# Later places for the steps of an attention unit, and smaller, spread loads of the down stage's tables, in a pooled-attention and two-MLP kernel

## The chip, the cores and the metric

The kernel runs on one core of a Trainium2 chip. The metric is device time in microseconds, here 1985.22 us as the median of three runs. A core has five engines with one instruction queue each, and each queue is worked off in order: TensorE (PE, with its weight loads as PEld), VectorE (DVE), ScalarE (ACT), GpSimd (POOL) and SyncE (SP), which only issues DMAs here. An instruction that waits holds up everything behind it on its own engine.

## The reference

```
k_p, v_p = mean over 8 neighbouring keys        # 576 -> 72 keys, 8 batches x 8 heads, 64 wide
a = softmax(q @ k_p.T / 8);  x = a @ v_p        # x: 4608 tokens x 512
h = x @ w_in;  g = h * clip(h + 3, 0, 6) / 6    # w_in 512 x 2048
y = g @ w_out                                   # w_out 2048 x 512
out = (silu(y @ w_gate) * (y @ w_val)) @ w_out2 # 512 x 1536, 1536 x 512
```

Everything is float32; the weights come as 64-bit numbers that the kernel converts itself.

## The kernel before

A float32 product is made of three products of rounded parts: each operand is split into a high part (rounded by ACT) and a remainder (a subtraction by DVE).

The program has three stages. The **up stage** handles 9 blocks of 512 tokens. A block has 16 feature tiles f; each is one group of 12 matmuls (`up`, L579) into one of three PSUM buffers, an activation (`act1`: ACT `t`, DVE `g`, for f < 8 also GpSimd), and a store of g (256 KB) to DRAM (`store_g`). The **down stage** (L838, 63 products in a seven-product scheme) reads g and seven tables of w_out, 2 MB each (`load_pw`), and the **last stage** (L663 and behind) does the second MLP.

While block j runs in the up stage, the attention of block j+1 is computed between the groups of matmuls, and the attention of block 0 runs ahead of them. So blocks 0 to 7 carry attention, and block 8 carries none. Attention is cut into 96 units (a head pair and up to 256 queries). The steps of a unit are letters:

- S: scores on PE into PSUM (`pss`), row maximum on DVE. X (`exps`): DVE subtracts the maximum into the tile `e`, and ACT takes the exponential. N: DVE adds the rows up and inverts the sums. M: GpSimd multiplies them in. E: ACT rounds the last columns into `et`, and DVE (odd units) or GpSimd (even ones) subtracts.
- T: PE transposes into PSUM (`pst`, two buffers). U: ACT rounds that into `aT`, `aTt`. L: DVE makes the remainder.
- V: four products on PE into `psv`, which has one buffer. W: ACT rounds it into `x`. Y: DVE makes the remainder, which frees `psv` for the next unit's V.
- Per head: RK and K (pooled keys, by GpSimd and then PE and ACT), R0, R1 and R (pooled values). Per segment of queries: P.

A table `when` gives each step a pair (d, p): unit i does it in unit interval i + d, at place p of the interval. All steps are sorted by that into one list, `steps`. The list is cut in front of its S, V and T steps into 30 pieces per block, and two pieces follow each group of 12 matmuls: one ahead of `act1`, one behind it (`attn_slot`). Each engine's queue is written in this order. Where blocks 0 and 1 are concerned (`early_units`), ACT subtracts the maximum itself. At the end of feature tiles, `prep_slot` adds the preparation of later tables, 20 of them within blocks 1 to 7: for each, at the ends of several feature tiles, ACT rescales, DVE joins halves of words, GpSimd adds (L202), ACT rounds (L261), DVE subtracts (L264).

In the last block the loads for the down stage are put on SP's queue ahead of the block's first group: g of block 0 (4 pieces of 1 MB) and two tables; four more tables follow at f = 3, 7, 11 and 15, the last at the end. The stores of g stand on the same queue.

Of the kernel before, what the change touches and what calls it, by code (L numbers as in the profile page):

```python
# [9 lines left out]
F32R = mybir.dt.float32r  # L10
# [8 lines left out]
def f32(ap):  # L19
    return ap.bitcast(F32)  # L20
# [3 lines left out]
def kernel(  # L24
# [27 lines left out]
    nc = tc.nc  # L52
# [227 lines left out]

    attn_ctx = ExitStack()
    a_p = attn_ctx.enter_context(tc.tile_pool(name="a", bufs=1, side="right"))
    NE = 2
    MAXQ = 2
    QJ = N // P
    kbd_t = [a_p.tile([P, K2], F32, name=f"kbd{p}") for p in range(KT)]
# [172 lines left out]
        qT_t[seg] = t.rearrange("p c s -> p (c s)")  # L459

    n_unit = [0]
    s_t, ps_t, x_ps = {}, {}, {}

    def scores(u):
        b, p, s0, n, qt = u
# [14 lines left out]
    def exps(u):  # L480
        b, p, s0, n, qt = u
        ni = n // qt
        g = ni * 2
        s3, mx, st = s_t.pop(u)
        if st:
            e = es_t[0][:, MAXQ * K2 * (n_unit[0] % 3):][:, :MAXQ * K2]
            e = e.rearrange("q (i s) -> q i s", i=MAXQ)[:qt, :ni]
        else:
            e = a_p.tile([P, MAXQ, K2], F32, tag="e", name="e", bufs=NE)[:qt, :ni]
        e3 = e.rearrange("q i (h s) -> q (i h) s", h=2)  # L490
        sm = a_p.tile([P, 2 * MAXQ, 1], F32, tag="sm", name="sm", bufs=3)[:qt, :g]
        if u in early_units:
            for i in range(g):
                nc.scalar.activation(
                    out=e3[:, i], in_=s3[:, i], func=ACTF.Exp, bias=mx[:, i], accum_out=sm[:, i]
                )
        else:
            nc.vector.tensor_tensor(  # L498
                out=e3, in0=s3, in1=mx.to_broadcast([qt, g, SP_]), op=ALU.subtract
            )  # L500
            nc.scalar.activation(out=e, in_=e, func=ACTF.Exp)  # L501
        e_t[u] = (e, e3, et_t[n_unit[0] % NE][:qt, :ni], sm)
        n_unit[0] += 1

    def normalise(u):
        _, e3, _, sm = e_t[u]
# [87 lines left out]
            nc.gpsimd.tensor_tensor(out=g[:, MB:], in0=g[:, :MB], in1=g[:, MB:], op=ALU.subtract)  # L594
        return g

    def store_g(j, f, g):
        nc.sync.dma_start(out=g_d[j][:, :, f // NP1, f % NP1], in_=g.rearrange("p (r n) -> p r n", r=2))

# [200 lines left out]
            t = gq[j, slot] = lb["gq"].tile([P, NP1, MB], F32, tag=f"gq{slot}", name="gq")  # L800
            nc.sync.dma_start(out=t, in_=g_d[j][:, r, c])

    def load_pw(n, tile_of):
        what = DN[n][2]
        t = tile_of("pw")
        lb["pw", what] = t.rearrange("p (f a n) -> p f a n", f=NP1, a=2)
        nc.sync.dma_start(out=f32(t), in_=s_w1[:, B7[what]].rearrange("p f a n -> p (f a n)"))

    SLOT = {"11": 0, "S1": 0, "12": 1, "S4": 1, "S3": 2, "22": 3, "S2": 3}

# [74 lines left out]
    for j in range(NB):  # L885
# [28 lines left out]

    when_startup = {
# [3 lines left out]
    }  # L919
    when = {  # L920
# [3 lines left out]
    }  # L924
    events = []
    for i in range(NU):
        startup_unit = i < unit_end[0]
        lag = dict(when_startup if startup_unit else when)
        if 0 <= i - unit_end[0] < NE:
            lag["E"] = (1, 22)  # L930
        if i == unit_end[0]:
            lag["V"], lag["W"] = (3, 10), (3, 11)
        stages = [(what, i) for what in "SXNMETULVWY"]
        if 2 <= i < 8:
            stages.append(("C", i))
        if i in first_in_seg:
            stages.append(("P", first_in_seg[i]))
        if i in first_in_head:
            stages += [(what, first_in_head[i]) for what in ("RK", "K", "R0", "R1", "R")]
        events += [(i + lag[st[0]][0], lag[st[0]][1], st[1], st) for st in stages]  # L940
    steps = [e[3] for e in sorted(events, key=lambda e: e[:3])]
    block_end = [1 + steps.index(("Y", e - 1)) for e in unit_end]


# [11 lines left out]

    for i, u in enumerate(units):
        h, sg = head_no[u[:2]], seg_no[seg_of[u]]
        before(*((what, i) for what in "SXNMETULVWY"))
        before(("P", sg), ("S", i))  # L960
        before(("RK", h), ("K", h), ("S", i))
        before(("R0", h), ("R", h), ("V", i))
        before(("R1", h), ("R", h))
        if i + 1 < NU:
            for what in "SXE":
                before((what, i), (what, i + 1))
        if h + 4 < len(heads):
            before(("S", i), ("K", h + 4))
            before(("V", i), ("R", h + 4))
        if h + 1 < len(heads):  # L970
            before(("K", h), ("RK", h + 1))
        if h + 2 < len(heads) and h >= KT - 1:
            before(("R", h), ("R1", h + 2))
        in_startup = at["S", i] < block_end[0]
        ring(*(("h", 3) if in_startup else ("att", 2)), ("S", i), ("X", i))
        assert not in_startup or at["X", i] < block_end[0]
# [6 lines left out]
        ring("mx", 2, ("S", i), ("X", i))  # L983
        ring("sm", 3, ("X", i), ("M", i))
# [16 lines left out]
    def do_step(st):  # L1001
        what, i = st
        if what == "RK":
            if i not in pe_pooled:
                reduce_k(*heads[i])
                next_k(i)
        elif what == "K":
            transpose_k(*heads[i])
            if i in pe_pooled:
                next_k(i)  # L1010
        elif what == "R0":
            prep_v(*heads[i])
        elif what == "R1":
            pool_v(vt_t[heads[i]])
        elif what == "R":
            split_v(*heads[i])
            for h in ((KT, KT + 1) if i == KT - 1 else (i + 2,)):
                if KT <= h < len(heads) and i >= KT - 1:
                    load_vtail(*heads[h], nc.sync)
            for h in ((KT, KT + 1) if i == KT - 1 else (i + 2,)):  # L1020
                if KT <= h < len(heads) and i >= KT - 1:
                    load_v(*heads[h], nc.sync)
        elif what == "P":
            prep_q(segs[i])
            for n in ((KT, KT + 1) if i == KT - 1 else (i + 2,)):
                if KT <= n < len(segs) and i >= KT - 1:
                    later.append((done[0] + 12, lambda n=n: load_q(segs[n], sync4)))
        elif what == "S":
            scores(units[i])
        elif what == "N":  # L1030
            normalise(units[i])
        elif what == "X":
            exps(units[i])
        elif what == "M":
# [28 lines left out]
    with tc.manual_schedule():  # L1063
# [43 lines left out]
        def load_next():  # L1107

            if sent[0] < NG * len(stream):
                kind, what = stream[sent[0] % len(stream)]  # L1110
                (load_up if kind == "up" else load_dn)(what)
                sent[0] += 1

        for j in range(NB):
            for f in range(F1):
                if (j, f) == (NB - 1, 0):
                    attn_ctx.close()
                    for nm in ("gq", "px"):
                        lb[nm] = right_b.enter_context(
                            tc.tile_pool(name=nm, bufs=1, side="right", reuse_waits="tile"))  # L1120
                    load_g(0, 0)
                    load_pw(0, lambda name: lb["px"].tile([P, BIG], F32R, tag="px", name=name))
                    load_pw(1, big_x)
                    for slot in (3, 2, 1):
                        load_g(0, slot)
                hp = ps_h.tile([P, N], F32, tag="h", name="h")
                up(hp, wu[f], x_tile(j))
                attn_slot(j, 2 * f)
                g = act1(f, hp)
                attn_slot(j, 2 * f + 1)  # L1130
                store_g(j, f, g)
                if j == 0:
                    weights.convert()
                else:
                    prep_slot(F1 * (j - 1) + f)
                if j == NB - 1:
                    if f % 4 == 3:
                        load_pw(2 + f // 4, big_w)
                    if 10 <= f < 10 + NCB:
                        split_b(0, f - 10)  # L1140
        load_pw(6, big_x)
        l1.close()
        l1_ps.close()
        lb["o"] = left_b.enter_context(tc.tile_pool(name="ob", bufs=1, reuse_waits="tile"))
# [91 lines left out]
```

## Time and profile before

| | us |
|---|---|
| median of 3 runs (1984.73 to 1987.58) | 1985.22 |
| the profiled execution: its time, its span | 1987.09, 1985.4 |
| up stage with attention, blocks 0 to 7 | 53.3 to 755.4 |
| up stage, block 8 | 755.4 to 818 |
| down stage and last stage | 818 to 1985.4 |

The stretches are read from the starts of the first groups of L579 in blocks 0 and 8, and from the first matmul of the down stage. Times in a trace count from the start of the span.

### The profile page before, as it was taken

The page shows a single profiled execution, that of the slowest core. Times are in us where ns is not written, and L with a number is a line of the kernel's source. Part 1 is how long each engine was busy: PE and PEld are TensorE (multiplying, and loading weights), DVE is VectorE, ACT ScalarE, POOL GpSimd, SP SyncE. Part 2 cuts the span into 40 slices and gives each one's busy share as a digit, 9 for nine tenths or more (in the row PEclk, how much of TensorE's full clock was granted, in tenths as well). Part 3 has the DMA queues.
Part 4 walks back from the last instruction along what each step waited for, and adds up shares of the span by engine and source line. Part 5 has one row for each costly group of instructions (what it writes and reads, how often), then busy time and mean ns, then how long its engine had stood idle before and what let it go on. Part 6 is the DMA issues. An engine that isn't in the chain of part 4 may idle for free.

```text
span 1985.4 us, 31395 instructions
## 1 busy us (share of the span) xinstructions
PE 1781.0 (90%) x11241; PEld 1663.1 (84%) x11241; DVE 1346.6 (68%) x2398; ACT 761.5 (38%) x1689; POOL 690.7 (35%) x898
## 2 busy tenths in 40 slices
PE   5877678786777876999999989999999999999999
PEld 4666566565656665999999989999999999999999
DVE  6666666665667652488788776676866867768666
ACT  5443334343434342445555542332422423324223
POOL 5436374646464431000000005515335155153360
PEclk8888989998988888999999999999999999999999
DMA  7635555756464648856455537788797787887876
GB/s 170 157 104 148 170 171 179 223 184 187 159 177 164 187 152 317 279 210 215 168 170 192 201 145 254 244 292 282 243 321 259 266 300 245 294 286 242 289 246 221
DMA packets 234828, 432.52 MB, mean 218 GB/s; under 512 B 86576, under 2 KB 168496, under 8 KB 218416
## 3 DMA queue, kind: packets, MB, share of 16 engines
q1 hardware_dynamic: 232528, 429.20, 65.0%
q8 instruction: 89, 1.46, 0.3%
q10 hardware_dynamic: 2144, 1.31, 0.2%
q14 instruction: 67, 0.55, 0.1%
HBM read 326.11 MB, written 104.33 MB: 217 GB/s over the span
## 4 chain that ended last, share of the span: by engine, by line
PE 69%; DVE 9%; DMA 6%; POOL 6%; ACT 6%; issue 4%; SPq 1%; POOLq 0%; DVEq 0%; ACTq 0%
PE b L663 40%; PE b L838 18%; PE h L579 9%; POOL e L514 2%; DMA g<-g 1%; DVE g L592 1%; DMA q_in<-in_q_dram 1%; ACT t L590 1%; DVE x L572 1%; DVE mx L477 1%; POOL vts L425 1%; DMA qv<-in_q_dram 1%; DVE sm L508 1%; POOL k_in L382 1%; ACT s L261 1%
## 5 line engine op out<-in xcount | busy, mean ns | idle before, releaser
L663 PE MATMUL b<-xc,wr 128*128 128x384 f32 x3024 | 529.5, 336 | 7.7 <-DMA wr<-sup 3.3
L663 PEld LDWEIGHTS b<-xc,wr 128*128 128x128 f32 x3024 | 527.2, 189 | 8.8 <-ACT xc L144 7.0
L579 PE MATMUL h<-x,wu 128*128 128x512 f32 x1728 | 477.6, 433 | 19.0 <-DVE g L592 16.9
L579 PEld LDWEIGHTS h<-x,wu 128*128 128x128 f32 x1728 | 355.2, 212 | 96.0 <-DVE g L592 17.9
L710 POOL TENSOR_TENSOR s<-s,c 128x384 f32<-128x384 f32 x144 | 142.4, 1014 | 763.3 <-ACT s L708 763.3
L672 DVE TENSOR_TENSOR c<-c,b 128x384 f32<-128x384 f32 x504 | 265.2, 552 | 179.0 <-PE b L663 155.3
L838 PEld LDWEIGHTS b<-gb,pw 128*128 128x128 f32 x3024 | 362.3, 191 | 0.4 <-DVE gb L145 0.2
L838 PE MATMUL b<-gb,pw 128*128 128x256 f32 x3024 | 362.6, 283 | 0.0
L663 PE MATMUL b<-wr,gc 128*128 128x256 f32 x2268 | 265.6, 279 | 0.0
L663 PEld LDWEIGHTS b<-wr,gc 128*128 128x128 f32 x2268 | 265.4, 188 | 0.0
L144 ACT CAST gb<-gq 128x512 fp32r<-128x512 f32 x252 | 155.9, 622 | 172.6 <-PE b L838 157.3
L145 DVE TENSOR_TENSOR gb<-gq,gb 128x512 fp32r<-128x512 f32 x252 | 168.6, 689 | 72.9 <-ACT gb L144 71.6
L717 POOL TENSOR_TENSOR gf<-s,c 128x384 f32<-128x384 f32 x144 | 168.3, 1193 | 66.9 <-DVE c L672 64.4
L592 DVE SCALAR_TENSOR_TENSOR g<-t,h 128x512 f32<-128x512 f32 x144 | 98.6, 685 | 134.0 <-ACT t L590 97.3
L144 ACT CAST gc<-gf 128x768 fp32r<-128x768 f32 x126 | 105.7, 839 | 186.9 <-POOL gf L717 101.0
L708 ACT ACTIVATE s<-c 128x384 f32<-128x384 f32 x144 | 73.5, 526 | 204.6 <-DVE c L672 203.3
L557 PE MATMUL psv<-aT,vst 128*128 128x256 f32 (+3 forms) x96 | 34.8, 362 | 123.7 <-DVE x L572 118.4
L514 POOL TENSOR_TENSOR e<-e,sm 96x288 f32<-96x288 f32 (+3 forms) x85 | 57.8, 680 | 251.4 <-DVE sm L510 221.5
L145 DVE TENSOR_TENSOR gc<-gf,gc 128x768 fp32r<-128x768 f32 x126 | 133.8, 1094 | 15.6 <-ACT gc L144 13.9
L557 PEld LDWEIGHTS psv<-aT,vst 128*128 128x128 f32 x96 | 20.9, 218 | 138.7 <-issue 61.4
L590 ACT ACTIVATE t<-h,half 128x512 f32<-128x512 f32 x144 | 99.0, 688 | 54.7 <-PE h L579 54.5
L501 ACT ACTIVATE e<-e 96x288 f32<-96x288 f32 (+3 forms) x76 | 31.4, 413 | 191.4 <-DVE e L498 191.4
(106 smaller groups left out, 1864.7 us busy)
## 6 DMA issues: line engine op xcount, KB each, us to landing
wr<-sup SPq DMA_DIRECT2D x72, 1024.0 KB
wr<-sdn SPq DMA_DIRECT2D x84, 768.0 KB
wr<-sup SPq DMA_DIRECT2D x72, 768.0 KB
g<-g SPq DMA_DIRECT2D x144, 256.0 KB
gq<-g SPq DMA_DIRECT2D x36, 1024.0 KB
sup<-s SPq DMA_DIRECT2D x12, 1792.0 KB
wstg<-in_moe_w_out_dram SPq DMA_DIRECT2D x56, 256.0 KB
sw<-s SPq DMA_DIRECT2D x8, 1792.0 KB
```

The costliest lines, as they stand in the source:

```text
L144: nc.scalar.copy(out=hi, in_=src)
L145: lo_engine.tensor_tensor(out=lo, in0=src, in1=f32(hi), op=ALU.subtract)
L514: nc.gpsimd.tensor_tensor(out=e3, in0=e3, in1=sm.to_broadcast(list(e3.shape)), op=ALU.mult)
L579: nc.tensor.matmul(out=ps, lhsT=w(kt, wh), rhs=x(kt, xh), start=first and n == 0, stop=last and n == 3 * len(kts) - 1,)
L590: nc.scalar.activation(out=t, in_=ps, func=ACTF.Relu, bias=half, scale=1.0 / 6.0)
L592: nc.vector.scalar_tensor_tensor(out=g, in0=t, scalar=1.0, in1=ps, op0=ALU.min, op1=ALU.mult)
L663: nc.tensor.matmul(out=ps, lhsT=w(wh), rhs=x(xh), start=first and n == 0, stop=last and n == 2)
L672: add = lambda dst, a, b: nc.vector.tensor_tensor(out=dst, in0=a, in1=b, op=ALU.add)
L708: nc.scalar.activation(out=g[q], in_=c[q], func=ACTF.Sigmoid)
L710: nc.gpsimd.tensor_tensor(out=g[q], in0=g[q], in1=c[q], op=ALU.mult)
L717: nc.gpsimd.tensor_tensor(out=gf[p][:, GP[TURN[q]], f], in0=g[q], in1=c[q], op=ALU.mult)
L838: nc.tensor.matmul(out=ps[:, d], lhsT=w[:, CB * c + k, wh, P * d:P * (d + 1)], rhs=g[:, gh, k], start=what == place and (c, d, k, m) == (0 ...
```

## The change

The exponential gets a step of its own, A, and the steps of a unit lie further apart: S to Y reached from (1, 0) to (3, 20), and now reaches from (1, 0) to (5, 20.5). The tile `e` (and `et`) gets a third buffer for it. The subtraction stays in X. The rest of the pairs in the table changes alike; R0, R1 and R come one interval later.

```diff
-    NE = 2
+    NE = 3
@@ exps(u): now ends with the subtraction
+        x_e[u] = e, e3, s3, mx
+        if u not in early_units:
+            nc.vector.tensor_tensor(
+                out=e3, in0=s3, in1=mx.to_broadcast([qt, g, SP_]), op=ALU.subtract
+            )
+
+    def exp_e(u):
+        e, e3, s3, mx = x_e.pop(u)
...
         else:
-            nc.vector.tensor_tensor(
-                out=e3, in0=s3, in1=mx.to_broadcast([qt, g, SP_]), op=ALU.subtract
-            )
             nc.scalar.activation(out=e, in_=e, func=ACTF.Exp)
@@ the table
-        "M": (1, 5), "E": (1, 12), "T": (2, 16), "U": (2, 17), "L": (2, 18), "V": (3, 14),
+        "M": (1, 19), "E": (2, 15), "T": (3, 16), "U": (4, 2), "L": (4, 15), "V": (5, 14),
...
@@ the main loop
+        first_loads = dict(enumerate([
+            ("g", 0, 0), ("w", 0, 0), ("w", 0, 1), ("g", 0, 3), ("w", 1, 0), ("w", 1, 1), ("w", 2, 0),
+            ("w", 2, 1), ("g", 0, 1), ("w", 3, 0), ("w", 3, 1), ("g", 0, 2)]))
...
-                    load_g(0, 0)
-                    load_pw(0, lambda name: lb["px"].tile([P, BIG], F32R, tag="px", name=name))
-                    load_pw(1, big_x)
-                    for slot in (3, 2, 1):
-                        load_g(0, slot)
+                    new_pw(0, lb["px"].tile([P, BIG], F32R, tag="px", name="pw"))
+                    new_pw(1, big_x("pw"))
+                    late = []
...
-                store_g(j, f, g)
+                if j < NB - 1:
+                    store_g(nc.sync, j, f, g)
...
                 if j == NB - 1:
+                    for args in late:
+                        store_g(nc.scalar, *args)
+                    late = [(j, f, g)]
                     if f % 4 == 3:
-                        load_pw(2 + f // 4, big_w)
-                    if 10 <= f < 10 + NCB:
-                        split_b(0, f - 10)
-        load_pw(6, big_x)
+                        new_pw(2 + f // 4, big_w("pw"))
+                    if f in first_loads:
+                        kind, *args = first_loads[f]
+                        (load_g if kind == "g" else load_pw)(*args)
+                    if f >= F1 - NCB:
+                        split_b(0, f - F1 + NCB)
+        store_g(nc.scalar, *late[0])
+        new_pw(6, big_x("pw"))
+        for n in (4, 5, 6):
+            for h in range(2):
+                load_pw(n, h)
```

`load_pw` now moves half a table (1 MB), and in block 8 at most one load of 1 MB is written per feature tile. The stores of block 8 go to ACT's DMA queue, each one feature tile later.

ACT's queue in the middle of block 4, before; names with one number belong to one unit. `t` is the activation of a group of matmuls, `e_4945 <- e_4945` the exponential, `et0 <- e_4945` the rounding E of the same unit, `x` is W, `aT` and `aTt` are U:

```order
L568 CAST x_4220<-psv_4887 128x192
L544 CAST aT_4920<-pst_4915 128x192
L545 CAST aTt_4921<-pst_4915 96x192
L144 CAST vst3_126<-v_in_4765 128x128
L441 ACTIVATE vtl3_130<-vts1_132 96x64
L590 ACTIVATE t_4936<-h_4902,half_91 128x512
L501 ACTIVATE e_4945<-e_4945 96x288
L521 CAST et0_134<-e_4945 96x2x2x16
L568 CAST x_4220<-psv_4957 128x192
```

The exponential and the rounding of the same tile `e_4945` are neighbours. The same place with the change:

```order
L598 ACTIVATE t_4934<-h_4905,half_91 128x512
L576 CAST x_4255<-psv_4938 128x192
L529 CAST et1_135<-e_4856 96x2x2x16
L509 ACTIVATE e_4928<-e_4928 96x288
L598 ACTIVATE t_4978<-h_4955,half_91 128x512
L552 CAST aT_4989<-pst_4968 128x192
L553 CAST aTt_4990<-pst_4968 96x192
L576 CAST x_4255<-psv_4995 128x192
L529 CAST et2_136<-e_4928 96x2x2x16
L509 ACTIVATE e_4987<-e_4987 96x288
```

E is now that of the unit before (`e_4928`, whose exponential stands five rows higher), and both stand behind W.

DVE's queue at the same place, before: `mx` is the maximum, `e <- pss,mx` the subtraction, the three `sm` rows are N, `aT` is L, `x` is Y:

```order
L477 TENSOR_REDUCE mx_4943<-pss_4940 96x4
L498 TENSOR_TENSOR e_4945<-pss_4940,mx_4943 96x288
L458 STREAM_TRANSPOSE qT_4949<-q_in_4768 128x384
L508 TENSOR_REDUCE sm_4946<-e_4945 96x4
L509 TENSOR_SCALAR sm_4946<-sm_4946 96x4
L510 RECIPROCAL sm_4946<-sm_4946 96x4
L551 TENSOR_TENSOR aT_4992<-pst_4987,aT_4992 128x192
L572 TENSOR_TENSOR x_4220<-psv_4957,x_4220 128x192
```

N follows its own subtraction, and L and Y come last. With the change:

```order
L477 TENSOR_REDUCE mx_4985<-pss_4982 96x4
L494 TENSOR_TENSOR e_4987<-pss_4982,mx_4985 96x288
L458 STREAM_TRANSPOSE qT_4993<-q_in_4755 128x384
L559 TENSOR_TENSOR aT_4989<-pst_4968,aT_4989 128x192
L532 TENSOR_TENSOR et2_136<-e_4928,et2_136 96x2x16
L516 TENSOR_REDUCE sm_5004<-e_4987 96x4
L517 TENSOR_SCALAR sm_5004<-sm_5004 96x4
L518 RECIPROCAL sm_5004<-sm_5004 96x4
L580 TENSOR_TENSOR x_4255<-psv_4995,x_4255 128x192
```

L and E now stand between the subtraction and N, and L reads a transpose (`pst_4968`) that stands one unit further back.

SP's queue as block 8 begins, before (`sup` is a prepared table, `gq` and `pw` are the loads, `g_101` the stores of block 8):

```order
L266 DMA sup_114<-s_7408 128x3584
L801 DMA gq<-g_93 128x2048
L807 DMA pw<-sw_102 128x4096 x2
L801 DMA gq<-g_93 128x2048 x3
L598 DMA g_101<-g_7464 256x1x256
L598 DMA g_101<-g_7483 256x1x256
```

All four pieces of g and two whole tables stand ahead of the stores. With the change:

```order
L266 DMA sup_114<-s_7410 128x3584
L809 DMA gq<-g_93 128x2048
L816 DMA pw<-sw_102 128x2048 x2
L809 DMA gq<-g_93 128x2048
L816 DMA pw<-sw_102 128x2048 x4
L809 DMA gq<-g_93 128x2048
```

No store of block 8 stands on SP's queue any more; the 16 stores stand on ACT's, each behind the `t` of the next feature tile.

## Rows read from the trace of the kernel before

**Rows 1.** Windows: us, busy us (count) by engine, PEclk, DMA share, GB/s.

```profile
53.30:755.40 702.10, 548.97 (x2610) 447.68 (x2610) 445.91 (x1000) 285.62 (x816) 345.26 (x541) 0.89 0.56 170
755.40:818.00 62.60, 46.95 (x195) 38.27 (x194) 15.20 (x21) 13.08 (x22) 5.83 (x8) 0.86 0.87 318
818.00:1985.40 1167.40, 1155.65 (x8316) 1154.09 (x8314) 847.27 (x1278) 432.32 (x716) 310.71 (x288) 0.99 0.70 244
```

**Rows 2.** Windows of line L579 alone: us, PE, PEld, PEclk, DMA share, GB/s.

```profile
53.30:755.40 702.10, 430.63 (x1536) 317.12 (x1537) 0.89 0.56 170
```

**Rows 3.** Waits, 53.3 to 755.4 us: total us, times, longest.

```profile
ACT e L501 <- DVE e L498: 191.4, 74, 5.4
ACT et L521 <- POOL e L514: 144.9, 85, 5.0
PE psv L557 <- DVE x L572: 118.4, 54, 6.8
DVE g L592 <- ACT t L590: 80.6, 61, 4.6
DVE aT L551 <- ACT aTt L545: 62.3, 26, 6.6
...
DVE et L524 <- ACT et L521: 46.9, 43, 2.2
...
PE psk L406 <- POOL kp L382: 31.0, 16, 4.4
```

**Rows 4.** Timeline, 721 to 747 us: start, us, instruction, [idle before <-releaser].

```profile
729.30 0.44 ACT L501 ACTIVATE e<-e 128x288 f32<-128x288 f32 x1 [4.04 <-DVE e L498]
729.78 0.46 DVE L508 TENSOR_REDUCE sm<-e 128x4 f32<-128x288 f32 x1 [0.51 <-ACT e L501]
729.85 3.00 PE L579 MATMUL h<-x,wu 128*128 128x512 f32 x12
...
730.82 0.67 POOL L514 TENSOR_TENSOR e<-e,sm 128x288 f32<-128x288 f32 x1 [5.08 <-DVE sm L510]
731.52 0.25 ACT L521 CAST et<-e 128x64 fp32r<-128x64 f32 x1 [1.78 <-POOL e L514]
731.67 0.36 ACT L568 CAST x<-psv 128x256 fp32r<-128x256 f32 x1
...
731.93 0.69 ACT L590 ACTIVATE t<-h,half 128x512 f32<-128x512 f32 x1
732.05 2.91 POOL L202 TENSOR_TENSOR q<-q 128x256 f32<-128x256 f32 x4
...
732.71 0.69 DVE L592 SCALAR_TENSOR_TENSOR g<-t,h 128x512 f32<-128x512 f32 x1 [2.06 <-ACT t L590]
...
734.99 1.68 ACT L261 CAST s<-q 128x1792 fp32r<-128x1792 f32 x1 [2.37 <-POOL q L202]
...
737.25 0.42 DVE L551 TENSOR_TENSOR aT<-pst,aT 128x256 fp32r<-128x256 f32 x1 [3.85 <-ACT aTt L545]
737.59 0.41 DVE L572 TENSOR_TENSOR x<-psv,x 128x256 fp32r<-128x256 f32 x1
...
738.15 0.55 PE L557 MATMUL psv<-aT,vst 128*128 128x256 f32 x1 [5.30 <-DVE x L572]
...
742.09 2.02 DVE L264 TENSOR_TENSOR s<-q,s 128x1792 fp32r<-128x1792 f32 x1
```

**Rows 5.** Timeline, 745 to 830 us, the last block.

```profile
752.67 19.22 PE L579 MATMUL h<-x,wu 128*128 128x512 f32 x84
...
759.99 2.16 SPq L807 DMA_DIRECT2D pw<-sw  x2
...
764.85 23.98 SPq L598 DMA_DIRECT2D g<-g  x4
...
786.79 2.04 DVE L592 SCALAR_TENSOR_TENSOR g<-t,h 128x512 f32<-128x512 f32 x3 [21.62 <-DMA g<-g]
...
787.54 30.42 PE L579 MATMUL h<-x,wu 128*128 128x512 f32 x120 [15.65 <-DVE g L592]
```

**Rows 6.** The page's costliest groups: busy us, mean ns | idle before.

```profile
L838 PE MATMUL b<-gb,pw 128*128 128x256 f32 x3024 | 362.6, 283 | 0.0
```

More of the change, by code (lines that the diff above doesn't have):

```diff
@@ L461 @@
     n_unit = [0]
-    s_t, ps_t, x_ps = {}, {}, {}
+    s_t, ps_t, x_ps, x_e, n_exp = {}, {}, {}, {}, [0]
     def scores(u):
@@ L487, in exps @@
             e = e.rearrange("q (i s) -> q i s", i=MAXQ)[:qt, :ni]
+            n_unit[0] += 1
         else:
@@ L490, in exps @@
         e3 = e.rearrange("q i (h s) -> q (i h) s", h=2)
+        x_e[u] = e, e3, s3, mx
[5 more added lines that the diff above has]
+        e, e3, s3, mx = x_e.pop(u)
+        qt, ni = e.shape[0], e.shape[1]
+        g = ni * 2
         sm = a_p.tile([P, 2 * MAXQ, 1], F32, tag="sm", name="sm", bufs=3)[:qt, :g]
@@ L497, in exps @@
         else:
-            nc.vector.tensor_tensor(
-                out=e3, in0=s3, in1=mx.to_broadcast([qt, g, SP_]), op=ALU.subtract
-            )
             nc.scalar.activation(out=e, in_=e, func=ACTF.Exp)
-        e_t[u] = (e, e3, et_t[n_unit[0] % NE][:qt, :ni], sm)
-        n_unit[0] += 1
+        e_t[u] = (e, e3, et_t[n_exp[0] % NE][:qt, :ni], sm)
+        n_exp[0] += 1
     def normalise(u):
@@ L595, in act1, with store_g @@
         return g
-    def store_g(j, f, g):
-        nc.sync.dma_start(out=g_d[j][:, :, f // NP1, f % NP1], in_=g.rearrange("p (r n) -> p r n", r=2))
+    def store_g(eng, j, f, g):
+        eng.dma_start(out=g_d[j][:, :, f // NP1, f % NP1], in_=g.rearrange("p (r n) -> p r n", r=2))
     UP = [("P1", "11", "11"), ("P6", "S2", "T2"), ("P5", "S1", "T1"), ("P2", "12", "21"),
@@ L801, in load_g, with new_pw, load_pw @@
             nc.sync.dma_start(out=t, in_=g_d[j][:, r, c])
[L803 to L807, printed above, removed]
+    def new_pw(n, t):
+        lb["pw", DN[n][2]] = t.rearrange("p (f a n) -> p f a n", f=NP1, a=2)
+    def load_pw(n, half):
+        what, fs = DN[n][2], slice(NP1 // 2 * half, NP1 // 2 * (half + 1))
+        nc.sync.dma_start(
+            out=f32(lb["pw", what][:, fs]).rearrange("p f a n -> p (f a n)"),
+            in_=s_w1[:, B7[what], fs].rearrange("p f a n -> p (f a n)"),
+        )
     SLOT = {"11": 0, "S1": 0, "12": 1, "S4": 1, "S3": 2, "22": 3, "S2": 3}
@@ L928 @@
         lag = dict(when_startup if startup_unit else when)
[L929 to L933, printed above, removed]
+        if units[i] in early_units and not startup_unit:
+            lag["A"] = (1, 1)
+        stages = [(what, i) for what in "SXANMETULVWY"]
         if 2 <= i < 8:
@@ L939 @@
             stages += [(what, first_in_head[i]) for what in ("RK", "K", "R0", "R1", "R")]
-        events += [(i + lag[st[0]][0], lag[st[0]][1], st[1], st) for st in stages]
-    steps = [e[3] for e in sorted(events, key=lambda e: e[:3])]
+        events += [(i + lag[st[0]][0], lag[st[0]][1], st[1], n, st) for n, st in enumerate(stages)]
+    steps = [e[4] for e in sorted(events, key=lambda e: e[:4])]
     block_end = [1 + steps.index(("Y", e - 1)) for e in unit_end]
@@ L958 @@
         h, sg = head_no[u[:2]], seg_no[seg_of[u]]
-        before(*((what, i) for what in "SXNMETULVWY"))
+        before(*((what, i) for what in "SXANMETULVWY"))
         before(("P", sg), ("S", i))
@@ L964 @@
         if i + 1 < NU:
-            for what in "SXE":
+            for what in "SXAE":
                 before((what, i), (what, i + 1))
@@ L974 @@
         in_startup = at["S", i] < block_end[0]
-        ring(*(("h", 3) if in_startup else ("att", 2)), ("S", i), ("X", i))
-        assert not in_startup or at["X", i] < block_end[0]
+        freed = "A" if u in early_units else "X"
+        ring(*(("h", 3) if in_startup else ("att", 2)), ("S", i), (freed, i))
+        assert not in_startup or at[freed, i] < block_end[0]
         ring("yt", 2, ("T", i), ("L", i))
@@ L982 @@
             ring("e", NE, ("X", i), ("T", i))
-        ring("mx", 2, ("S", i), ("X", i))
-        ring("sm", 3, ("X", i), ("M", i))
+        ring("mx", 2, ("S", i), (freed, i))
+        ring("sm", 3, ("A", i), ("M", i))
         ring("et", NE, ("E", i), ("T", i))
@@ L1033, in do_step @@
             exps(units[i])
+        elif what == "A":
+            exp_e(units[i])
         elif what == "M":
```

6 rows, old and new, of tables (when, when_startup) are left out of this document.

## The prediction

> **What bounds the kernel now.** I first cut the span into stretches with the windows [rows 1]. From 818 us on PE is busy for 1155.65 of 1167.40 us at a clock of 0.99, and nothing of the change stands there, so these 1167 us stay. From 53.3 to 755.4 us, blocks 0 to 7, PE is busy 549.0 of 702.1 us. No other engine is full there: DVE 445.9, GpSimd 345.3, ACT 285.6. So 153 us of PE's time are waits on a chain, and the granted clock of 0.89 says that part of the busy time ran at the lower of the two levels (1.2 GHz) too. Block 8, 62.6 us with 47.0 busy, has no attention and still waits.
>
> The waits [rows 3] name the chain. PE stood 118.4 us ahead of the first product of V, and 31.0 us ahead of K. Further up the chain ACT stood 191.4 us ahead of the exponential and 144.9 us ahead of the rounding E, both in the middle of its queue. The timeline [rows 4] shows how that reaches PE. At 729.30 ACT takes the exponential and then can do nothing: the rounding E of the same unit needs the sums on DVE (729.78) and the product on GpSimd (730.82), so ACT idles 1.78 us until 731.52. GpSimd, held until then by its own wait of 5.08 us, starts the four additions of a table's preparation only at 732.05; ACT's rounding L261 waits for them until 734.99 and takes 1.68 us; the roundings U stand behind it, DVE's L (737.25) and Y (737.59) behind those, and PE, which had finished its groups, has waited 5.30 us when V starts at 738.15. That is the pattern: a step that waits for its own unit holds a queue, a long piece of a preparation falls behind it, and V, for which L and Y are due one or two pieces after T and V, has no room.
>
> The lower clock can be priced. One group of 12 takes 3.00 us at full clock [rows 4]; 128 groups would take 384 us, and L579 was busy 430.6 [rows 2], so 47 us too long. The rest of PE's work there, 549.0 - 430.6 = 118.4 us, is too long by 13 us if it shared the same ratio of 1.12. At the higher level PE's work in blocks 0 to 7 is thus some 489 us, or 5.6 us for each of the 88 units that have their V there.
>
> **The change, part by part.** *The steps further apart.* The number of instructions on PE, DVE and GpSimd is the same; the attention of a block is cut into pieces as before. What changes is how long ago an operand was made. U reads a transpose from half an interval before, L stands half an interval behind U, and V a whole interval behind L. E reads a product that was asked for in the interval before. So of the chain in [rows 4] the waits of ACT for E, and of DVE for `aTt`, lose their cause. What stays as a tight loop is `psv`, which has one buffer: V, W, (E), exponential, N, Y, next V. Its length from [rows 4] is 0.36 + 0.25 + 0.44 for ACT, 1.04 for N (from 729.78 to GpSimd's start at 730.82, its handover with it), 0.41 for Y, 0.55 for V, and an estimated 0.3 for the other handovers (Y's end at 738.00 to V at 738.15): 3.35 us. With `t` and `g` of a group in between (0.69 each) it is 4.7 us. PE's pace is 5.6 us a unit, so the loop has 1 to 2 us of room. A long piece of preparation (GpSimd 2.91, DVE 2.02, ACT 1.68 [rows 4]) takes this room whenever it falls into the loop. There are 20 preparations, each with four such pieces on ACT and DVE; where none falls in, the room covers them. Nothing left of 118.4 is one end, all of it the other. I take half, 59 us, which is 3 us a preparation: about what two pieces in the loop cost beyond their room.
>
> The 31.0 us ahead of K stay in the sum: RK and K keep their places. Their ends are 0 (GpSimd no longer held by M) and 62 (units follow each other faster, and RK on GpSimd does not).
>
> Clock: the 60 us (47 + 13) go with the waits, above all the long ones: after the 15.65 us in block 8 the next groups ran slow [rows 5], while the group at 729.85 took its 3.00 us amid short waits [rows 4]. I let 44 of the 60 come back, as a good part of the waits stays; the ends are 0 and 60.
>
> PE side: 702.1 - 59 - 44 = 599 us. From DVE's side: of its 256 us without work, 62.3 (L) should shrink to some 6, 46.9 (E) to some 20, since E is now half ready, and 80.6 (`g` for `t`) to some 60, because DVE runs behind PE more often: 702.1 - 56 - 27 - 20 = 599 as well. Both go by choice of the kept parts, between the floor of 489 us and 702.
>
> *The third buffer of `e`* costs no time; it is what lets A and E stand an interval apart. *R0, R1, R* come an interval later and keep their distance from V two intervals and more, so GpSimd's time for pooling is hidden by that. *Loads of q, k and v* keep their distance in steps; DMA engines were 56% busy [rows 1], which becomes 66% in 599 us. That covers them; without it each late q would cost some us, which I leave to the range.
>
> *Block 8.* SP queued a prepared table (1.8 MB), then 4 MB of g and 4 MB of tables (759.99), then the stores (764.85); the first store's buffer was free only at 786.79, after DVE had idled 21.62 us and PE 15.65 us [rows 5]. Behind it 120 matmuls took 30.42 us where 84 had taken 19.22 (2.74 us a group), so 3.0 us went to the clock. 16 groups at 2.74 are 43.8 us; 43.8 + 15.65 + 3.0 = 62.5, which is all of block 8. With the change the stores stand on ACT's queue, and on SP's the loads. ACT is busy 13 us of 62.6, so 16 issues of up to 1.1 us (two on SP took 2.16) lie in its idle time. A store is written one group late, and its buffer is needed again three groups on, so 5.5 us are left for it to land. Here 1.8 + 8.4 million bytes were gone in the 27 us from 760 to 787, 0.38 MB a us; a store of 0.26 MB that shares with the loads half and half needs 1.4 us plus its latency. I allow 1.5 us of remaining waits: 45.3 us, 17.3 less. Loads: 12 MB are asked for within the block, 6 of them at once; at 0.38 MB a us beside 4 MB of stores that is 44 us, just the length of the block. The last tables come behind that, but they serve the fifth product on, and the 63 products take 362.6 / 63 = 5.8 us each [rows 6], so there are 23 us of cover.
>
> A rule speaks against this part. The row shows that stores behind 8 MB on the same queue waited for them. The Trainium skill, "DMA: Bandwidth & Descriptors", section "Issuing engines are not separate DMA queues", says that DMAs started by different engines run on the same 16 engines and interleave, and that starting them elsewhere saves only the issue time. Read strictly, block 8 would keep its 15.7 us; read by its word "interleave", a store need not wait for all that SP queued before. No row here has loads and stores on two queues.
>
> Sum: 103 + 17 = 120 us off the profiled execution's 1987.1 is 1867; the median of the runs lies 1.9 us lower, so 1865 us.
>
> **Rivals.** (a) *The wait moves instead of going.* With A behind W, N waits for V of the same interval, so DVE is tied to PE once per unit, and preparations hit the loop as they hit the old chain. For it: DVE has 446 us of work at a pace of 489, so it can't catch up quickly. Against it: ACT's 336 us of waits in two places [rows 3] lose their cause. Then only block 8 and a fifth of the rest come: 1985 - 17 - 20 = 1948.
>
> (b) *All of it comes.* If the room of the loop swallows the preparations, PE falls to its work of 489 us plus K's 31 and some 15 us: 535 us, and the total to 1985 - 167 - 17 = 1801. DVE's 446 us of work allow it only if it hardly ever waits.
>
> (c) *The stores still wait.* The DMA engines take the loads in order ahead of the stores wherever these come from: block 8 keeps 16 us and the total is 1881. The rule named above, in its strict reading, is this case.
>
> (d) *Slower.* The place is N on DVE: it now stands behind L and E, and waits for an exponential that stands behind W, thus behind V on PE. If that handover (PE to ACT to DVE to PE) takes more than PE's pace, each unit pays. PE now loses 118.4 / 88 = 1.35 us a unit; the kernel gets slower once it loses 1.35 + 17 / 88 = 1.54 us. At 1.8 us the total is 1985 + 40 - 17 = 2008. That needs a loop of 7.4 us, against 4.7 reckoned.
>
> (e) That the change does nothing can be left out, since ACT's and DVE's orders are shown to differ.
>
> **How the numbers follow.** Forecast 0.53 (own range 1830 to 1905), (a) 0.20, (b) 0.11, (c) 0.08, (d) 0.08. A measurement tells 0.2%, some 4 us, from no change. All but (d) are faster, less a small part of (a) near no change: faster 0.89, same 0.03, slower 0.08. The range leaves out (d), the upper third of (a), and the lower half of (b): 1808 to 1950. It takes in K's wait at 0 or 62 us.
>
> **What would show it.** In the changed kernel's windows, blocks 0 to 7 should take some 600 us with a clock over 0.93, block 8 some 45. PE's wait ahead of V should be near 60 us, with DVE's Y or the exponential's chain as its releaser; ACT's wait for E near 20 us; DVE's wait for `aTt` near 6. K's wait tells whether GpSimd has become the limit. In block 8 no `g` should wait for a store longer than 2 us. I am wrong if V still waits 100 us or more (then a), if K's wait has grown past 60 (GpSimd), or if block 8 still shows a wait of 10 us or more (c).

## The result and the profile after

The changed kernel takes 1893.11 us (median of four runs, 1890.54 to 1894.82) against 1984.97 us: a ratio of 0.953, 95% interval 0.952 to 0.955. That is 92 us less where 120 were forecast, inside the range. Blocks 0 to 7 carry 86 of it and block 8 carries 9.

Windows of the changed kernel, the same four stretches as in [rows 1] with the start-up ahead; columns as there. The span is 1891.3 us, the profiled execution 1893.08.

```profile
0.00:50.90 50.90, 28.14 (x122) 21.46 (x123) 35.35 (x94) 29.94 (x136) 28.32 (x62) 0.77 0.73 173
50.90:667.40 616.50, 519.52 (x2613) 428.36 (x2613) 436.43 (x1005) 283.13 (x819) 350.56 (x541) 0.92 0.64 194
667.40:721.30 53.90, 47.03 (x196) 37.61 (x195) 12.82 (x18) 12.12 (x18) 5.79 (x8) 0.94 0.91 341
721.30:1891.30 1170.00, 1155.68 (x8316) 1154.02 (x8314) 849.46 (x1282) 433.10 (x718) 310.67 (x288) 0.99 0.71 244
```

Blocks 0 to 7 fell from 702.1 to 616.5 us (forecast 599), block 8 from 62.6 to 53.9 (forecast 45.3). The rest is 2.6 us longer and the start-up 2.4 us shorter. PE's work is the same, but it was busy 519.5 instead of 549.0 us: 29.5 us came back through the clock, and 56 us of waits went. Two of the signs named ahead did not come: the granted clock of blocks 0 to 7 is 0.92 and not over 0.93, and in block 8 `g` waits up to 8.6 us for a store where 2 us were named.

Waits of the changed kernel, 50.9 to 667.4 us, against [rows 3]; lines behind the changed places have moved by some numbers (V is L565, the exponential L509, E L529, L559 is L).

```profile
ACT x L576 <- PE psv L568: 110.4, 68, 4.1
DVE g L600 <- ACT t L598: 89.2, 64, 3.9
...
PE psv L565 <- DVE x L580: 80.5, 37, 7.4
...
ACT e L509 <- DVE e L494: 27.5, 20, 3.6
...
DVE et L532 <- ACT et L529: 13.3, 8, 3.9
...
DVE qT L458 <- DMA q_in<-in_q_dram: 10.1, 4, 4.8
...
PE psk L406 <- POOL kp L382: 8.7, 6, 2.4
...
ACT et L529 <- POOL e L522: 5.3, 3, 2.1
...
DVE aT L559 <- ACT aTt L553: 2.6, 2, 1.6
```

ACT's two waits in the middle of its queue fell from 191.4 and 144.9 us to 27.5 and 5.3. What ACT now waits for is W (110.4 us), thus V, which PE has just been given: that is ACT being early, not late. DVE's wait for `aTt` fell from 62.3 to 2.6 us. PE's own waits fell from 118.4 to 80.5 us ahead of V and from 31.0 to 8.7 ahead of K.

A wait that stays, in the timeline of the changed kernel around 571 us:

```profile
570.79 0.24 DVE L458 STREAM_TRANSPOSE qT<-q_in 128x64 f32<-128x64 f32 x1 [3.64 <-DMA q_in<-in_q_dram]
...
571.87 0.83 DVE L136 TENSOR_SCALAR q<-wstg 128x512 int32<-128x512 int32 x1
...
577.12 0.36 DVE L580 TENSOR_TENSOR x<-psv,x 128x192 fp32r<-128x192 f32 x1
...
577.53 0.58 PE L565 MATMUL psv<-aT,vst 128*128 128x256 f32 x1 [6.71 <-DVE x L580]
```

DVE first waits 3.64 us for queries still in flight, then has the joins of a preparation (from L136 on), sums, and remainders of pooled values, and only at 577.12 comes to Y; PE has waited 6.71 us for it. Late loads, which I had left to the range, show up once units follow each other faster.

Block 8 of the changed kernel, timeline:

```profile
673.06 0.58 ACTq L606 DMA_DIRECT2D g<-g  x1
...
684.45 0.32 SPq L809 DMA_DIRECT2D gq<-g  x1
684.55 0.69 DVE L600 SCALAR_TENSOR_TENSOR g<-t,h 128x512 f32<-128x512 f32 x1 [7.37 <-DMA g<-g]
684.87 13.62 SPq L816 DMA_DIRECT2D pw<-sw  x4
...
686.09 0.52 ACTq L606 DMA_DIRECT2D g<-g  x1
...
697.20 1.28 DVE L600 SCALAR_TENSOR_TENSOR g<-t,h 128x512 f32<-128x512 f32 x2 [8.57 <-DMA g<-g]
697.95 18.93 PE L587 MATMUL h<-x,wu 128*128 128x512 f32 x72 [4.13 <-DVE g L600]
```

`g` waits up to 8.6 us at a time for a store. It has three buffers, so the `g` at 684.55 is the fourth and waits for the first store, issued at 673.06, and the one at 697.20 is the seventh and waits for the fourth, issued at 686.09: each lands some 11 us after its issue, not after 1.4 us plus a latency. By the semaphores in the trace, the 13 stores issued from 673 to 719 us landed 3.6 to 11.4 us after their issue, in the middle 9.2. PE waits 6.9 us in all there.

The loads of this block are not spread as the program text suggests. With the stores gone from SP's queue nothing there waits for a feature tile any more, and SP asks for its loads in three bursts, at 671 to 673, 684 to 698 and 706 to 708 us.

### The profile page after: what moved, and what is told of

Read it like the earlier page. It is cut to its first block, busy times and chain, and to the rows that moved or that the text cites. A ratio compares the mean times of both kernels' runs of the same rounds, so it can differ in the third digit from the quotient of the medians.

```text
span 1891.3 us, 31360 instructions
## 1 busy us (share of the span) xinstructions
PE 1750.4 (93%) x11241; PEld 1641.4 (87%) x11241; DVE 1334.1 (71%) x2398; ACT 758.3 (40%) x1689; POOL 695.3 (37%) x899
## 4 chain that ended last, share of the span: by engine, by line
PE 71%; DMA 8%; DVE 8%; POOL 4%; ACT 3%; SPq 3%; issue 3%; POOLq 0%; DVEq 0%; ACTq 0%
PE b L671 42%; PE b L850 17%; PE h L587 10%; DMA g<-g 3%; DMA q_in<-in_q_dram 2%; DVE g L600 2%; ACT t L598 1%; POOL vts L425 1%; SPq L366 1%; DMA wstg<-in_moe_w_out_dram 1%; POOL v_in L425 1%; POOL g L602 1%; POOL q L207 1%; SPq L118 1%; DMA wstg<-in_moe_w_gate_dram 1%
## 5 line engine op out<-in xcount | busy, mean ns | idle before, releaser
L587 PE MATMUL h<-x,wu 128*128 128x512 f32 x1728 | 458.8, 420 | 6.9 <-DVE g L600 6.9
L587 PEld LDWEIGHTS h<-x,wu 128*128 128x128 f32 x1728 | 340.7, 203 | 79.4 <-DVE g L600 8.3
L145 DVE TENSOR_TENSOR gc<-gf,gc 128x768 fp32r<-128x768 f32 x126 | 133.8, 1095 | 15.6 <-ACT gc L144 13.9
L565 PE MATMUL psv<-aT,vst 128*128 128x256 f32 (+3 forms) x96 | 32.6, 339 | 90.3 <-DVE x L580 80.5
L565 PEld LDWEIGHTS psv<-aT,vst 128*128 128x128 f32 x96 | 19.6, 204 | 101.3 <-DVE x L580 31.6
L602 POOL TENSOR_TENSOR g<-g 128x256 f32<-128x256 f32 x72 | 57.1, 795 | 121.5 <-DVE g L600 112.3
L522 POOL TENSOR_TENSOR e<-e,sm 96x288 f32<-96x288 f32 (+3 forms) x85 | 58.8, 692 | 106.6 <-DVE sm L518 69.9
```

The costliest lines, as they stand in the source:

```text
L145: lo_engine.tensor_tensor(out=lo, in0=src, in1=f32(hi), op=ALU.subtract)
L587: nc.tensor.matmul(out=ps, lhsT=w(kt, wh), rhs=x(kt, xh), start=first and n == 0, stop=last and n == 3 * len(kts) - 1,)
```

## Experiments

All times are medians. The kernel before took 1986 to 1987 us beside them and 1985 us beside the change, so a difference of 1 or 2 us from the change says nothing.

**Block 8 alone, and the steps alone.** The first kernel is the one before with the new block 8, the second the changed one with the old block 8; the edits are given in short.

```diff
+ first_loads, load_pw in halves, store_g(nc.scalar, ...) one feature tile late   # e1: put into the kernel before
- the same                                                                        # e2: taken out of the changed kernel
```

> The kernel before with the changed block 8 alone (loads of 1 MB spread over feature tiles, stores on ACT's queue), steps of attention as before. If the two parts add up, this takes what block 8 lost in the changed kernel's trace (62.6 to 53.9 us) less the 2.6 us that the rest of the program got longer: about 6 us less than before, 1979 us. If block 8 was only so slow in the changed kernel because attention ended differently there, it gives the predicted 17 us, 1968.

> The changed steps of attention with the old block 8 (whole tables and all of g on SP's queue ahead of the stores). If the parts add up: 1893 + 6 to 9 = 1899 to 1902 us, with blocks 0 to 7 at 616 us as in the changed kernel and block 8 back at 62 us with one wait of some 16 us. If the steps needed the new block 8, blocks 0 to 7 would differ from 616.

Block 8 alone: 1981.47 us against 1986.19, ratio 0.998 (0.997 to 0.999), 4.7 us less. The steps alone: 1897.77 us, ratio 0.956 (0.954 to 0.957), 88.4 less. Together 93, the change itself 92: the two parts add up, and the steps are nearly all of it. The steps alone leave blocks 0 to 7 at 616.3 us and block 8 at 61.3, with one wait of PE of 15.5 us, as the sum requires. With block 8 alone changed, block 8 fell from 62.4 to 55.8 us and the stretch behind it grew by 2.9, as it grew by 2.6 in the change; why it grows is open.

**The exponential ahead of V.**

```diff
-"X": (1, 1), "A": (1, 15),
+"X": (1, 1), "A": (1, 10),
```

> The changed kernel with the exponential A at place 10 instead of 15, thus in the piece ahead of V and not behind W. Theory 1 (the loop V, W, E, exponential, N, Y, next V is what PE still waits in): the exponential leaves the loop, about 1 us per unit, so PE's wait ahead of V falls from 80 to 50 us or less and the total to 1860 to 1875. Rival (long pieces of preparation, value pooling and late loads hold DVE and ACT wherever the exponential stands): within 6 us of 1893, and ACT's wait for the subtraction grows from 28 us.

1909.46 us, 16 us slower than the change (ratio to before 0.961, 0.960 to 0.962). Waits of this kernel, blocks 0 to 7:

```profile
ACT e L509 <- DVE e L494: 184.2, 75, 6.5
...
PE psv L565 <- DVE x L580: 90.1, 41, 7.7
```

Theory 1's numbers did not come, and PE waits longer; nor did the rival's total come, though its sign did, the growing wait for the subtraction. ACT now stands 184 us ahead of the exponential, as it did before the change, and W, behind it, comes late: ACT's wait for V there fell from 110.4 to 11.9 us. The exponential belongs behind W, where its input is ready; that place alone is worth 16 us of the 88. Whether the loop sets PE's pace is not decided by this run, because it takes the exponential out of the loop and puts a wait in front of W, which is part of it.

**Loads of q earlier.**

```diff
-                    later.append((done[0] + 12, lambda n=n: load_q(segs[n], sync4)))
+                    later.append((done[0] + 2, lambda n=n: load_q(segs[n], sync4)))
```

> The changed kernel with the loads of q written 2 steps behind P instead of 12. Late loads as a cause: DVE's wait for q_in (10.1 us in 4 waits, one of them ahead of a wait of PE of 6.7 us) goes, and the total falls by 5 to 10 us to 1883 to 1888. Preparation as the only cause: no change beyond 3 us.

1886.56 us, 6.5 us faster than the change (0.950, 0.948 to 0.951). DVE's wait for queries fell from 10.1 to 4.3 us. Late loads are a part of what stays, a small one.

**Fewer loads within block 8.**

```diff
-            ("w", 2, 1), ("g", 0, 1), ("w", 3, 0), ("w", 3, 1), ("g", 0, 2)]))
+            ("w", 2, 1), ("g", 0, 1)]))
```

> The changed kernel with 9 instead of 12 loads of 1 MB in block 8; one table and the last piece of g are asked for behind it. If block 8 (53.9 us at 341 GB/s, DMA engines 91% busy) is held by the DMA engines, it falls to some 48 us and the total by 3 to 6 us, unless the product that needs the late table then waits. If the stores wait for something else (order of semaphores, ACT's issue), block 8 stays at 53 to 55 us.

1893.80 us (0.953, 0.952 to 0.955): no difference from the change, and block 8 took 55.7 us. But the edit did not do what it was meant to do. SP's queue has no store in this block, so the three loads written behind the block stand on it in the same order as before, and SP asked for them at the same point, well before the block's end at 723.6 us:

```profile
707.02 0.32 SPq L809 DMA_DIRECT2D gq<-g  x1
707.78 0.79 SPq L816 DMA_DIRECT2D pw<-sw  x2
708.62 0.74 SPq L809 DMA_DIRECT2D gq<-g  x1
```

In the changed kernel it is 706.89 and 707.73 for the last two rows. So this run is no test, and whether fewer bytes in the block would shorten it stays open.

**Stores of block 8 back on SP.**

```diff
-                if j < NB - 1:
-                    store_g(nc.sync, j, f, g)
+                store_g(nc.sync, j, f, g)
...
-                    for args in late:
-                        store_g(nc.scalar, *args)
-                    late = [(j, f, g)]
...
```

> The changed kernel with the stores of block 8 back on SP's queue, each in its own feature tile, the loads spread as in the change. If a queue of its own is what helps the stores, block 8 gets longer than 53.9 us, up to the 62.6 us of before. If all DMAs share the same engines and only the size of what is asked for ahead of a store counts, block 8 is 51 to 56 us and the total within 4 us of 1893.

1883.02 us, 10 us faster than the change (0.948, 0.947 to 0.950). Block 8 of this kernel in the windows:

```profile
663.90:708.50 44.60, 44.33 (x195) 36.01 (x194) 12.94 (x18) 12.56 (x19) 5.90 (x8) 1.00 0.95 377
```

It moves 16.8 MB at 377 GB/s, where the changed kernel moved 18.4 MB at 341, at full clock, and PE waits 0.2 us. So neither named case holds: the queue of its own did not help the stores. They do not land at once here either. By the semaphores in the trace a store lands 0.7 us after the load in front of it, but 5.8 to 9.1 us after its own issue, in the middle 8.5, against 9.2 and at most 11.4 in the changed kernel. `g` waits in small, even portions (22.5 us in nine waits, at most 3.8), and with three PSUM buffers between them PE hardly notices. In the changed kernel it waits 32.4 us in six, up to 8.6, and that reaches PE: of the 9.3 us between the two kernels' blocks some 6.7 are PE's waits and 2.7 the clock.

Several things had changed at once, though. On one queue the loads are also paced, since SP cannot run ahead of the store in front of it. And a store is written in its own feature tile. For the first eight, which GpSimd works on as well, this matters little: the first is issued 5.2 us after the block's first matmul, against 5.7 in the changed kernel. For the others it is up to 2.6 us.

**Queues exchanged.** The loads go to ACT's queue, paced by ACT's activations, and the stores stay on SP's.

```diff
-            nc.sync.dma_start(out=t, in_=g_d[j][:, r, c])
+            (nc.scalar if j == 0 else nc.sync).dma_start(out=t, in_=g_d[j][:, r, c])
...
-        nc.sync.dma_start(
+        (nc.scalar if n < 4 else nc.sync).dma_start(
...
-                if j < NB - 1:
-                    store_g(nc.sync, j, f, g)
+                store_g(nc.sync, j, f, g)
...
```

> The changed kernel with stores and loads of block 8 on exchanged queues: the first 12 loads on ACT's queue, where each stands behind the activation of its feature tile, the stores on SP's, each in its own feature tile. With the stores back among the loads on SP, block 8 had fallen to 44.6 us. Theory A (SP ran ahead with the loads; what helps is that a load is asked for only when its feature tile is reached): block 8 is 44 to 47 us here too, the total about 1883. Theory B (two queues at once make a store land late, whichever carries what): block 8 stays at 52 us or more, the total at 1890 or more.

1894.76 us (0.954, 0.953 to 0.955), block 8 58.7 us. Timeline of this kernel:

```profile
669.78 17.73 SPq L606 DMA_DIRECT2D g<-g  x4
670.25 0.33 ACTq L816 DMA_DIRECT2D pw<-sw  x1
...
685.48 0.69 DVE L600 SCALAR_TENSOR_TENSOR g<-t,h 128x512 f32<-128x512 f32 x1 [11.11 <-DMA g<-g]
```

A load is asked for once per feature tile here too, and yet the first store, issued at 669.78, frees its buffer only at 685.48. Pacing alone is thus not what helps, and theory B's numbers came. This store stands behind the prepared table (1.8 MB) on SP's queue, as it also does with all on SP. There the table landed 5.9 us and the store 5.8 us after their issue; here, beside the loads of the other queue, the table took 11.9 us and the store 15.6. The next two stores took 17.0 and 17.6 us, later ones 2.4 to 12.3. In both arrangements with two queues some stores thus land later than any does on one (9.1 us). What the shared semaphores of the last section do to this was not tried by itself.

**Eleven preparations left out**, in the changed kernel and in the one before. The last stage uses one prepared table for all, so the output leaves these products out.

```diff
     for u in range(len(preps)):
...
+        if 9 <= u < 20:
+            continue
...
-        src = s_up[f][m].rearrange("p s a k f -> p s (a k f)")
+        src = s_up[0][0].rearrange("p s a k f -> p s (a k f)")
```

> The changed kernel without 11 of the 12 preparations of the tables of w_gate and w_val (those that lie in blocks 4 to 7); the last stage uses the one prepared table for all, so the output leaves those products out. Blocks 0 to 3 stay at 330 us. If preparations are what PE still waits for, blocks 4 to 6 lose most of their 40 us of waits: 237 us fall to some 195 to 205, and the total by 35 to 45 us. If it is value pooling and late loads, they fall by 10 us or less.

> The kernel before without the same 11 preparations; the output leaves the same products out. Blocks 4 to 7 took 347.6 us there. If the old order let a preparation fall on a queue that was held by its own unit's chain, these cost more here than in the changed kernel: the total falls by 60 to 90 us (against 35 to 45 in the changed kernel), so the two kernels come closer together. If the old order lost time by itself, without preparations, the fall is about the same in both and the distance of 92 us stays.

Changed: 1859.19 us, 34 less than with them (0.935, 0.934 to 0.937 of before). Before: 1924.55 us, 62 less (0.969, 0.967 to 0.970). Windows of the two over blocks 4 to 6, the changed kernel first:

```profile
379.60:586.60 207.00, 189.28 (x980) 156.36 (x979) 140.36 (x371) 84.98 (x279) 117.87 (x202) 0.96 0.45 127
```

```profile
406.40:643.90 237.50, 200.61 (x975) 163.31 (x974) 138.39 (x373) 86.71 (x279) 117.07 (x202) 0.92 0.40 112
```

With the preparations, blocks 4 to 6 of the changed kernel took 237.7 us with PE busy for 197.2. So 22.8 of 40.5 us of waits went, and 17.7 stay with only the end of one preparation there: 207 us, a little above the 195 to 205 expected. PE's wait ahead of V over blocks 0 to 7 fell less than the total did:

```profile
PE psv L567 <- DVE x L582: 61.9, 34, 5.9
```

It was 80.5 us, so eleven preparations account for 18.6 us of it, and 61.9 stay with nine preparations left.

In the total a preparation costs 62 / 11 = 5.6 us with the old steps and 34 / 11 = 3.1 with the new ones, the clock included. Some 4 to 6 us of either fall lie in block 8, which the left-out traffic relieves as well. The two kernels stay 65 us apart without these eleven; so the preparations are a part of the gain, 27 us for eleven, and not all of it.

**A part of the table at a time**, in the kernel before: E alone moved, and then all from U to Y moved and E left where it was. The third part, the exponential in a step of its own with N and M behind it, was not tried by itself, nor were the two parts together.

```diff
-        "M": (1, 5), "E": (1, 12), "T": (2, 16), "U": (2, 17), "L": (2, 18), "V": (3, 14),
-        "W": (3, 15), "Y": (3, 20),
+        "M": (1, 5), "E": (2, 13), "T": (2, 16), "U": (2, 17), "L": (2, 18), "V": (3, 14),   # e10
+        "W": (3, 15), "Y": (3, 20),
+        "M": (1, 5), "E": (1, 12), "T": (2, 16), "U": (3, 2), "L": (3, 15), "V": (4, 14),    # e11
+        "W": (4, 14.5), "Y": (4, 20.5),
...
-        if 0 <= i - unit_end[0] < NE:                 # e10
-            lag["E"] = (1, 22)
-        if i == unit_end[0]:                          # e11
-            lag["V"], lag["W"] = (3, 10), (3, 11)
```

> The kernel before with one step moved: E, the rounding that waits for the unit's own product, goes from the interval of the exponential to the next, ahead of V and T. If ACT held by this wait (144.9 us in 85 waits) was the main loss, ACT's wait for it falls below 30 us, PE's wait ahead of V from 118 to some 70, and the total to 1925 to 1945. If it only was the last of several tight places, the total stays above 1965.

> The kernel before with the other part of the table: U, L, V, W and Y half an interval to an interval later, while exponential, N, M and E keep their old places and E its wait. If the short distance from the transposes to V was the main loss, PE's wait ahead of V falls to 60 us or less and the total to 1920 to 1940. If a held ACT delays V however far it stands, PE's wait stays above 95 us and the total above 1960.

E alone: 1968.44 us, 18 less than before (0.992, 0.990 to 0.994). U to Y alone: 1989.22 us, ratio 1.002 (1.001 to 1.003), nothing gained. Waits with E alone moved:

```profile
PE pst L535 <- POOL et L524: 54.1, 29, 5.1
...
PE pst L535 <- DVE et L524: 30.9, 17, 4.0
PE psv L557 <- DVE x L572: 30.1, 22, 2.9
```

and with U to Y alone moved:

```profile
ACT et L521 <- POOL e L514: 125.5, 85, 5.3
PE psv L557 <- DVE x L572: 104.1, 39, 5.8
```

With E freed, PE's wait ahead of V is down to 30 us, but now T stands right behind E, and PE waits 85 us there. With V given room, ACT is still held in front of E, and V still waits 104 us. Either part alone mostly moves the wait.

**Both single gains on top of the change.**

```diff
+                    later.append((done[0] + 2, lambda n=n: load_q(segs[n], sync4)))
...
+                store_g(nc.sync, j, f, g)
...
```

> The changed kernel with both edits that gained alone: loads of q 2 steps behind P (6.5 us), stores of block 8 on SP's queue in their own feature tile (10 us). They lie in different stretches, so they should add up: 1876 to 1878 us.

1877.94 us, ratio 0.946 (0.944 to 0.947), 15 us faster than the change. It is the fastest version found.

## Why the prediction was right, and where its terms were off

*The stretch from 818 us on stays.* Right, to 2.6 us.

*Held queues as the cause.* Right: ACT's wait for E and DVE's wait for `aTt` went as reckoned (to 5.3 and 2.6 us), and the steps alone make 88 of 92 us. The single runs show what I had not seen: none of the waits tried by itself was the cause. With the change in place, giving ACT its wait at the exponential back (184 of 191 us) costs 16 us; in the kernel before, taking its wait for E away gains 18, and room for U to Y alone gains nothing. These pieces leave more than half of the 88 us, which only the steps together have given here. Which of them must move together was not taken apart.

*What is left ahead of V.* I took 59 us of 118; it is 80.5. I had charged all that stays to the 20 preparations, at 3 us of wait each. That was wrong in kind: eleven of them account for 18.6 us of this wait, 1.7 each (the 3.1 us each in the total hold the clock and block 8 as well), and 61.9 us stay without them. Late queries stand in it too: with earlier loads of q it is 73.8. The larger part was not taken apart.

*The sum from DVE's side.* It gave 599 us as well, by choice of what is kept. Its waits for `aTt` and E fell further than I let them (to 2.6 and 13.3 us), but `g` waits 89.2 us for `t`, not 60; it had been 80.6.

*The loop as the tight place.* Not borne out. PE's wait ahead of V still ends with Y, but with the exponential taken out of the loop V, W, E, exponential, N, Y the kernel got slower by 16 us. Since W was held up in that run, it does not show what sets the pace. Rival (d), which took the loop to be longer than PE's pace, did not come.

*K's wait.* I kept 31.0 us and named 0 as an end; 8.7 stayed. GpSimd's wait ahead of the product M fell from 221.5 to 69.9 us in the same stretches, so RK behind it starts in time; that this is the cause is read from the traces, not tried.

*Clock.* 29.5 us came back where I let 44 (L587 was busy 411.9 us against 384 at full clock). The reason I gave for the part that stays is the waits, but PE's waits as a whole came out as forecast: 97 us are left, and the forecast leaves 94. So the amount of waiting does not explain it, and why less came back is open. In the windows of the changed kernel, blocks 4 to 6 and block 7, the lower clock and the waits do stand in the same blocks:

```profile
377.20:614.90 237.70, 197.21 (x979) 161.27 (x978) 180.04 (x410) 106.60 (x303) 158.01 (x234) 0.91 0.65 202
614.90:667.40 52.50, 52.50 (x266) 44.23 (x266) 36.99 (x70) 27.73 (x57) 19.83 (x27) 1.00 0.67 238
```

In sum, blocks 0 to 7 gave 85.6 us instead of 103: 21 less from V and 14 less from the clock, 22 more from K, and some 4 us of small waits that I had not carried. That the waits as a whole came out so close (56 us gone, 59 forecast) is luck: V's miss and K's miss cancel.

*Block 8.* This step failed in size: 8.7 us in its stretch and 4.7 in the total, not 17.3. The sentence that failed is that a store sharing with the loads half and half needs 1.4 us plus its latency. Packets of the changed kernel by queue (q1 is SP's with the loads, q10 ACT's with the stores; packets, MB, share of the 16 engines' time), first from 673 to 678 us, then from 679 to 684:

```profile
q1 hardware_dynamic: 148, 1.63, 99.1%
```

```profile
q1 hardware_dynamic: 258, 1.85, 88.3%
q10 hardware_dynamic: 256, 0.25, 14.1%
```

The first store was issued at 673.06. For 5.7 us no packet of ACT's queue ran; why is open. Then the two queues went one packet for one: 256 packets against 258, 46 of them small ones of 4 bytes, but 0.25 MB against 1.85, since a packet of g holds 1 KB and one of a load 8 KB. A store of 256 KB is 256 packets, 16 per engine. If each waits for one packet of 8 KB (0.31 us each in this trace), that is some 5 us, and the store's packets took 5.0 us, from 678.80 to 683.76. Both parts together are most of the 11.4 us seen, so the step had the share wrong and had nothing for the 5.7 us. On one queue a store stands between two loads and lands 0.7 us after the one in front of it.

That the engines alternate by packets is an inference from these counts. The Trainium skill, "DMA: Bandwidth & Descriptors", section "Queues, rings and completion order", says that an engine goes round its queues a packet at a time, and that a packet there typically holds 9 to 17 descriptors. The counts fit an alternation, but whether the profile counts the same thing as a packet is not shown, and no run here shows a single engine.

Rival (c) stood as near as my own step: PE's waits fell from 15.7 to 6.9 us, where I had 1.5 and the rival 16, and block 8 took 53.9 us between 45.3 and 62. The rule of the Trainium skill ("DMA: Bandwidth & Descriptors", section "Issuing engines are not separate DMA queues"), read strictly, is that rival; read by its word "interleave", it is what the packets from 679 to 684 us show. What made PE's waits fall is not separated, as fewer loads stood ahead of the stores and the stores had a queue of their own. With the stores left among the loads on one queue PE's waits are gone (0.2 us), so the second queue was not needed.

## What to carry to other kernels

Where engines with in-order queues pass a unit's work around, look for the instruction that waits for its own unit in the middle of a queue, and put the step of an older unit there; and try the neighbours in the chain together, because here each of two parts alone mostly moved the wait. A place behind an instruction that is early is better than one ahead of it that makes the engine wait. In this kernel small stores did better between the loads on one queue than on a queue of their own beside large loads, with the loads asked for one at a time. An edit that leaves the order on a queue as it was tests nothing.

## What the hardware showed that I had not expected

A second DMA queue did not free the stores from the loads: on the queue of the loads a store of 256 KB landed within 9.1 us and block 8 took 44.6 us at 377 GB/s, while with loads and stores on two queues, whichever carried which, some stores took 11.4 and up to 17.6 us, and the block took 53.9 and 58.7 us at 341 and 318 GB/s. Loads were also held by stores with which they share no data. Waits of SP's queue in the changed kernel, 660 to 725 us:

```profile
SPq L816 <- DMA g<-g: 24.9, 4, 12.6
SPq L809 <- DMA g<-g: 18.0, 2, 10.3
```

In the trace the DMAs of both queues use eight semaphores in turn, and each waits for the DMA that used its semaphore before: the load issued at 684.45 had waited for the store issued at 673.06. So a store that lands late also stops the loads that come next.
